# The first FFN layer of three batches by Strassen's seven products, two feature tiles at a time

## The chip, the cores and the metric

The kernel runs on one core of a Trainium2 chip. Its engines are TensorE (PE in the profile, with PEld for its weight loads), VectorE (DVE), ScalarE (ACT), GpSimd (POOL) and SyncE (SP, which issues most DMAs). Each engine takes its own instructions strictly in the order in which the program issues them, and semaphores order the engines among each other. The metric is the device time of one execution in microseconds (us), as the median of several runs.

## The reference: what is computed

For each of 8 batches with 8 heads, S = 512 tokens x of width 64 and 32 state rows are read crosswise, and the result goes through a gated two-layer network (FFN) with weights w_in (512 x 2048) and w_out (2048 x 512):

```python
scores = scale * np.matmul(x, state.transpose(0, 1, 3, 2))
a = np.exp(scores - scores.max(-1, keepdims=True))
a /= a.sum(-1, keepdims=True) + 1e-09
xread = np.matmul(a, state)
# sread: the same with x and state exchanged
x = concatenate([xread, sread], axis=2) as (B * (512 + 32), 512)
h = x @ w_in
g = h * np.cos(h)
return g @ w_out
```

Everything is 32-bit float.

## The kernel before

**The first layer of a batch's tokens.** The read `a @ state` and the multiplication by w_in are joined: `products` (L429) multiplies a batch's state by 512 columns of w_in and keeps the result as an `sw` tile of 128 x 2 x 512 (L433 to L440; two of them alive, four a batch, nt = 0 to 3). The attention weights, transposed, are `aT` of 128 x 2 x 512 (two blocks of 128 heads-and-states, 512 tokens). So the 2048 hidden features of a batch are 16 tiles of 128 features, f = 0 to 15, and tile f is `h = sw[:,0,cols].T @ aT[:,0] + sw[:,1,cols].T @ aT[:,1]`. This is `hidden` (L462), two matmuls into one of two PSUM banks (`hps`, two buffers):

```python
t.hp = hps.tile([P, S], F32, name="h")[:, 0:t.n]
for i in range(t.kn):
    nc.tensor.matmul(out=t.hp, lhsT=t.lhs(i), rhs=t.rhs(i),
                     start=(i == 0), stop=(i == t.kn - 1))
```

**The gate**, h times cos h, follows in four parts: `gate` (ScalarE, L472, rounds h to an integer), `gate2` (VectorE, L475, subtracts), `gate3` (ScalarE, L478, a sine), and `gate4` (VectorE, L484), which takes a slot of `g_all` (28 slots of 128 x 512, a list of free ones taken from the front and refilled at the back) and writes the gated tile there. The bank of `h` is free after `gate4`.

**The second layer** is already done by Strassen's products (in Winograd's form), over a *pair* of batches: phases 0 and 1 are the halves of the 16 tiles of the even batch, phases 2 and 3 those of the odd one. `output` (L603) issues the products of a tile, each two 32-bit matmuls into the banks MAIN or SIDE of `acc`; in phases 0 to 2, for two tiles of three, one product of the pair before is added (`pr.before.more(1)`: p7, then p4). In phases 2 and 3 the sums on the right side are made by `minus` (L490): those called `soon` on VectorE from the second pair on and on GpSimd in the first pair, the others on GpSimd; `sums` is issued after `gate4`, `sums2` later in the step. Finished banks are read by L534 (`plus`), L539 and L541; their stores (`later`, `go` in `store`: L548 sums, L555 transposes and a DMA from SP) follow one by one.

**The order of the work** is written out by hand: a loop over steps (L831), one tile a step, 128 tiles of tokens and then 16 of states. A step issues, in this order: `hidden`; TensorE's attention work of the step (`go(0)`); `gate`, `gate2`; more attention work on ScalarE and VectorE (`go(1)`, `go(3)`); `gate3`; one `later`; `gate4`; `sums`; the rest of attention (`go(2)`, `go(4)`); `blocks` on GpSimd (L816, the sums of w_out, steps 16 to 33); `sums2`; and last `output` of the tile three steps back (LAG, L827). `plan` (L740) puts the parts of the next batch's attention on the 16 steps of the present one: for an even batch from 2 on, transposes L294 in steps 1 and 2, scores (L312) in 5 with the maxima L326, spreading L332 and L349 in 6, L342 and the exponentials L353 and L358 in 7, sums in 8, L379 in 9, transposes L385 in 10, reads L402 in 11 and 12 with L412, and in 15 `keep2` (L418) and `keep3` (L423, which writes the states that were read into `sT`). The `products` of `sw` stand in steps 0, 4 and 9 for this batch, and in step 14 for the first quarter of the next (copied by ScalarE at L439).

**The state tiles** at the end multiply w_in by `sT` (256 columns of all batches) with the same `hidden` and `gate`.

The numbers L... are lines of this text:

Of the kernel before, what the change touches and what calls it, by code (L numbers as in the profile page):

```python
# [21 lines left out]
def kernel(  # L22
# [16 lines left out]
    NC = S // P  # L39
    T = S + Ns  # L40
    WC = 512
    scale = 1.0 / math.sqrt(D)

    consts = ctx.enter_context(tc.tile_pool(name="consts", bufs=1))
# [52 lines left out]

    stT = consts.tile([P, B, P], F32)  # L100

    def load_x(b):

# [111 lines left out]
    def convert_part(i, p):  # L215
# [20 lines left out]
        else:  # L236
            nc.gpsimd.tensor_tensor(bits, bits, e, op=ALU.add)  # L237

    sT = consts.tile([P, NK, B, Ns], F32)
    aT_of, sw_of = {}, {}

    class Attention:

# [4 lines left out]
        def __init__(self, b):  # L250
            self.b = b

            self.x_b, self.xT = x_b, xT
            self.spread, self.z2 = xT[:, 0:2], xT[:, 2:4]
            self.a2T = xT[:, 0:2].rearrange("p j (c m) -> p j c m", c=NC)

            self.i12 = small.tile([P, 2 * self.NB + 2], F32, name="i12")
            self.m1 = self.i12[:, 0:2 * self.NB].rearrange(
                "p (j t) -> p j t", j=2)
            self.i2 = self.i12[:, 2 * self.NB:]  # L260
            self.m2 = small.tile([P, 2], F32, name="m2")
            self.sr = small.tile([P, 2, D], F32, name="sr")
            self.aT = self.z1 = carry.tile([P, 2, S], F32, name="aT")
            aT_of[b] = self.aT

# [155 lines left out]

        def keep3(self):
            nc.scalar.activation(  # L423
                sT[:, :, self.b, :],
                at[1][:, 0:P].rearrange("p (k n) -> p k n", k=NK),
                func=ACTF.Copy, scale=1.0 / TWO_PI)


# [38 lines left out]

    def gate(t):  # L470
        t.q = msb.tile([P, S], F32, name="q")[:, 0:t.n]
        nc.scalar.activation(t.q.bitcast(I32), t.hp, func=ACTF.Copy, bias=0.25)  # L472
# [4 lines left out]
    def gate3(t):  # L477
        nc.scalar.activation(t.q, t.q, func=ACTF.Sin, bias=halfpi,  # L478
                             scale=-TWO_PI)

    def gate4(t):
        t.slot = g_free.pop(0)
        t.g = g_all[:, t.slot, 0:t.n]
        nc.vector.tensor_tensor(t.g, t.hp, t.q, op=ALU.mult)  # L484


# [189 lines left out]
    def tiles():  # L676
        pr = None
        for b in range(B):
            if b % 2 == 0:
                pr = Pair(b // 2, pr)  # L680
            for f in range(NF):
                t = Tile()
                t.b, t.f, t.pair = b, f, pr
                t.phase, t.i = b % 2 * 2 + f // NH, f % NH
                t.n, t.kn = S, 2
                c = slice(P * f % WC, P * f % WC + P)
                t.lhs = lambda i, b=b, nt=P * f // WC, c=c: (
                    sw_of[b, nt][:, i, c])
                t.rhs = lambda i, b=b: aT_of[b][:, i]
                yield t  # L690
        for n in range(NF):
            t = Tile()
            t.b, t.n_th, t.f = B, n, (n + NH) % NF
            t.pair, t.last_pair, t.phase = None, pr, None
            t.n, t.kn = B * Ns, NK
            cols = slice(P * t.f, P * t.f + P)
            t.lhs = lambda i, cols=cols: w_in[:, i, cols]
            t.rhs = lambda i: sT[:, i].rearrange("p b n -> p (b n)")
            yield t


# [38 lines left out]
    def plan(b):  # L740
        pe, x_act, y_act, x_dve, y_dve = [
            {s: [] for s in range(NF)} for _ in range(5)]

        def prod(s, b, nt, *bank):
            pe[s].append((b, "products", nt) + bank)
            if b == 1 and 0 < nt < 3:
                x_dve[s].append((b, "products_taken", nt) + bank)
            else:
                x_act[s].append((b, "products_kept", nt) + bank)

        def pairs(s, b, name, kept, i):
            pe[s] += [(b, name, i), (b, name, i + 1)]
            x_act[s].append((b, kept, i))
            y_act[s].append((b, kept, i + 1))

        def early(b, s):
            if b == 1:
                pairs(s[0], b, "tokens", "tokens_kept", 0)
                pairs(s[1], b, "tokens", "tokens_kept", 2)
            else:  # L760
                for k in range(NK):
                    to = (x_dve, y_dve)[k % 2]
                    to[s[k // 2]].append((b, "tokens_turned", k))
            pe[s[2]].append((b, "scores"))
            x_dve[s[2]].append((b, "max1"))
            x_dve[s[3]].append((b, "spread1"))
            y_dve[s[3]].append((b, "shift"))
            x_dve[s[4]].append((b, "max2"))
            y_act[s[4]].append((b, "exps"))
            x_dve[s[5]].append((b, "sums"))  # L770
            y_dve[s[5]].append((b, "spread1"))
            x_dve[s[6]].append((b, "norm1"))

        def late(b, s):
            pairs(s[0], b, "turn", "turn_kept", 0)
            pe[s[1]].append((b, "reads", 0))
            pe[s[2]].append((b, "reads", 1))
            x_dve[s[2]].append((b, "keep"))
            if len(s) > 3:
                turned(b, s[3])  # L780

        def turned(b, s):
            pe[s].append((b, "keep2"))
            x_act[s].append((b, "keep3"))


        if b == 0:
            pe[0].append((0, "products", 0, SIDE, HC, WC))
            y_dve[0] += [(0, "products_taken", 0, SIDE, HC, WC),
                         (0, "inverse2")]  # L790
            prod(7, 0, 2, SIDE)
            prod(11, 0, 3)
            prod(13, 1, 0, MAIN)
            late(0, (1, 2, 3, 4))
            early(1, (5, 6, 7, 8, 9, 10, 11))
            late(1, (12, 13, 14))
        else:
            bank = (SIDE,) if b == 1 else ()
            if b == 1:
                turned(1, 0)  # L800
            prod(0, b, 1, *[MAIN for _ in bank])
            prod(4, b, 2, *bank)
            prod(9, b, 3, *bank)
            if b + 1 < B:
                prod(14, b + 1, 0)
                early(b + 1, (1 + (b == 1), 2 + (b == 1), 5, 6, 7, 8, 9))
                late(b + 1, (10, 11, 12, 15))
        return pe, x_act, y_act, x_dve, y_dve
# [6 lines left out]
    def blocks(op, out_, a, b, r):  # L815
        nc.gpsimd.tensor_tensor(out_[:, r], a[:, r], b[:, r], op=op)  # L816
# [14 lines left out]
    for step, t in enumerate(all_tiles):  # L831
        s = step % NF
        if s == 0 and t.b < B:
            steps = plan(t.b)
        todo = [p[s] if t.b < B else [] for p in steps]

        def go(n):
            for p in todo[n]:
                part(*p)

        last, conv = conv_at.get(step - 1, -1), conv_at.get(step, -1)
        if step == B * NF + (0 if f64 else 8):
            fetch(N_LOADS + 2)
        if step == 4:
            warm(1, acc[MAIN][0])
        if step != 1:
            hidden(t)
        if step == 0:
            hidden(all_tiles[1])
            warm(3, acc[MAIN][0])  # L850
            gate(t)
            gate2(t)
            convert(3, "bcdf")
            convert(4, "1")
            go(0)
        else:
            go(0)
            if step == 5:
                states(1, acc[SIDE][1])
            gate(t)  # L860
            gate2(t)
            if step == 3:
                warm(4, acc[MAIN][0])
                part(0, "products", 1, SIDE)
            go(1)
            go(3)
            if step == 1:
                convert(4, "bcdf")
            elif last >= 0:
                convert(last, "bcdf")  # L870
            if conv >= 0 and not todo[1]:
                convert(conv, "1")
        gate3(t)
        if step == 3:
            part(0, "products_kept", 1, SIDE)
        if later:
            later.pop(0)()
        gate4(t)
        if conv >= 0 and todo[1] and step > 0:
            convert(conv, "1")  # L880
        if t.pair is not None:
            sums(t)
        if step == 6:
            states_kept(1, acc[SIDE][1])
        go(2)
        if conv >= 0:
            convert(conv, "2")
        go(4)
        if step in block_at:
            blocks(*block_at[step])  # L890
        if t.pair is not None:
            sums2(t)
        while len(line) >= (LAG if step >= 2 * NH else LAG + 1):
            output(line.pop(0))
        line.append(t)
# [32 lines left out]
```

## Time and profile before

| what | us |
|---|---|
| median of 4 runs (774.94 to 776.62) | 775.73 |
| the profiled execution, its own time | 774.7 |
| span of its trace | 772.9 |
| TensorE busy | 761.9 |
| VectorE busy | 414.6 |
| ScalarE busy | 305.7 |
| GpSimd busy | 177.4 |
| batches 2, 4, 6 (`hidden` of their first tile to that of the next batch's), each | 86.8 |
| batches 3 and 5, each | 83.3 |

The span is the time from the first to the last instruction of the traced execution; the 1.8 us around it are launch and end. A line of the groups reads: line, engine, operation, out<-in by the program's names, shapes, xcount | busy us, mean ns of one | idle time of the engine before them and what ended it. A line of the timeline reads: start, duration, engine, line, operation, names, shapes, xcount (instructions in a row are merged) and, in brackets, the idle time before it with its releaser. One 32-bit matmul of the program is two instructions in the trace.

### The profile page before, as it was taken

To read this page: it belongs to the slowest core of one execution; us is meant where nothing else is said; L and a number is where in the kernel's file an instruction comes from. 1 tells how busy PE (TensorE), PEld (TensorE's weight loads), DVE (VectorE), ACT (ScalarE), POOL (GpSimd) and SP (SyncE) were. 2 spreads that over 40 slices of the span, in tenths; PEclk is the share of its full clock that TensorE was granted. 3 is DMA by queue.
4 is the path that set the end of the run, shared out by engine and by line. 5 is a ranking of instruction groups with operands and counts; after the bars stand their busy time and mean duration, and the time that the engine had idled before them with its cause. 6 is when DMAs were issued, how large, how long until landed. Compare 5 with 4: busy or idle time off the path is not lost.

```text
span 772.9 us, 7528 instructions
## 1 busy us (share of the span) xinstructions
PE 761.9 (99%) x2664; PEld 340.2 (44%) x2664; DVE 414.6 (54%) x654; ACT 305.7 (40%) x484; POOL 177.4 (23%) x118
## 2 busy tenths in 40 slices
PE   8998999999999999999999999999999999999997
PEld 3443443434344434434444434444444444455554
DVE  5778786625554468535553658435634546431431
ACT  3888845422263225332342335332533333212112
POOL 2353377862000001640000002630000005510200
PEclk9999999999999999999999999999999999999999
DMA  8595461150104310330105111410100114000021
GB/s 244 170 277 206 129 94 25 21 89 1 27 1 87 50 28 14 55 69 1 28 4 105 28 27 23 86 29 0 28 1 9 23 24 137 0 0 15 14 42 41
DMA packets 161957, 43.49 MB, mean 56 GB/s; under 512 B 153920, under 2 KB 153920, under 8 KB 161920
## 3 DMA queue, kind: packets, MB, share of 16 engines
q1 hardware_dynamic: 161024, 42.49, 25.4%
q10 hardware_dynamic: 768, 0.39, 0.2%
q8 instruction: 21, 0.34, 0.2%
q14 instruction: 16, 0.13, 0.1%
q0 software_dynamic: 128, 0.13, 0.1%
HBM read 34.08 MB, written 8.91 MB: 56 GB/s over the span
## 4 chain that ended last, share of the span: by engine, by line
PE 94%; DVE 3%; ACT 1%; DMA 1%; issue 0%; POOL 0%; SPq 0%; POOLq 0%
PE o L528 50%; PE h L465 31%; PE at L312 4%; PE o L648 4%; PE at L402 2%; PE o L312 1%; PE at L385 1%; DMA x_b<-in_x_dram 1%; DVE i L326 0%; PE o L705 0%; DVE xT L332 0%; DVE w_out L232 0%; DMA s<-in_state_dram 0%; POOL w_out L237 0%; ACT s L226 0%
## 5 line engine op out<-in xcount | busy, mean ns | idle before, releaser
L465 PE MATMUL h<-aT,sw 128*128 128x512 f32 x512 | 241.0, 593 | 2.9 <-DVE g_all L484 2.4
L475 DVE TENSOR_TENSOR q<-q,h 128x512 f32<-128x512 int32 (+1 forms) x144 | 94.4, 656 | 273.6 <-ACT q L472 273.5
L528 PE MATMUL o<-g_all,w_out 128*128 128x512 f32 x512 | 236.4, 598 | 0.3 <-POOL w_out L237 0.3
L472 ACT ACTIVATE q<-h 128x512 int32<-128x512 f32 (+1 forms) x144 | 82.3, 571 | 345.3 <-PE h L465 345.2
L490 POOL TENSOR_TENSOR g_all<-g_all 128x512 f32<-128x512 f32 x80 | 112.7, 1433 | 440.8 <-DVE g_all L484 440.8
L528 PE MATMUL o<-g_all,s 128*128 128x512 f32 x384 | 177.3, 598 | 0.0
L465 PEld LDWEIGHTS h<-aT,sw 128*128 128x128 f32 x512 | 96.6, 190 | 125.8 <-issue 107.6
L528 PEld LDWEIGHTS o<-g_all,w_out 128*128 128x128 f32 x512 | 94.1, 190 | 124.5 <-issue 120.5
L478 ACT ACTIVATE q<-q,halfpi 128x512 f32<-128x512 f32 (+1 forms) x144 | 100.7, 700 | 82.3 <-DVE q L475 82.3
L484 DVE TENSOR_TENSOR g_all<-h,q 128x512 f32<-128x512 f32 (+1 forms) x144 | 94.1, 653 | 55.3 <-ACT q L478 53.5
L528 PEld LDWEIGHTS o<-g_all,s 128*128 128x128 f32 x384 | 70.8, 190 | 91.7 <-issue 90.0
L237 POOL TENSOR_TENSOR w_out<-w_out,s 128x1024 int32<-128x1024 int32 x10 | 23.9, 2391 | 77.1 <-DVE w_out L232 60.3
L490 DVE TENSOR_TENSOR g_all<-g_all 128x512 f32<-128x512 f32 x48 | 33.4, 697 | 1.6
L439 ACT COPY sw<-at 128x512 f32<-128x512 f32 x50 | 26.8, 589 | 10.0 <-PE at L312 10.0
L465 PE MATMUL h<-sT,w_in 128*128 128x256 f32 x128 | 30.2, 379 | 0.0
L648 PE MATMUL o<-w_out,g_all 128*128 128x512 f32 x64 | 29.6, 592 | 0.0
L465 PEld LDWEIGHTS h<-sT,w_in 128*128 128x128 f32 x128 | 24.3, 190 | 10.1 <-issue 6.5
L237 POOL TENSOR_TENSOR w_in<-w_in,s 128x1024 int32<-128x1024 int32 (+1 forms) x10 | 19.3, 1932 | 37.0 <-DVE w_in L232 22.0
L312 PE MATMUL at<-w_in,stT 64*32 64x512 f32 x400 | 27.2, 601 | 0.0
L534 DVE SCALAR_TENSOR_TENSOR held<-o,held 128x512 f32<-128x512 f32 x40 | 25.3, 676 | 3.3 <-PE o L528 3.3
L555 DVE STREAM_TRANSPOSE ot<-held 128x512 f32<-128x512 f32 x32 | 22.2, 693 | 0.0
L332 DVE STREAM_TRANSPOSE xT<-i 128x1024 f32<-128x1024 f32 x16 | 19.8, 1236 | 0.0
(79 smaller groups left out, 405.3 us busy)
## 6 DMA issues: line engine op xcount, KB each, us to landing
out_dram<-ot SPq DMA_DIRECT2D x132, 64.0 KB, 2.0
g_all<-in_moe_w_out_dram SPq DMA_DIRECT2D x8, 1024.0 KB, 4.9
g_all<-in_moe_w_in_dram SPq DMA_DIRECT2D x6, 1024.0 KB, 5.3
xT<-in_x_dram SPq DMA_DIRECT2D x96, 64.0 KB, 2.3
x_b<-in_x_dram SPq DMA_DIRECT2D x24, 256.0 KB, 4.5
x_b<-in_x_dram SPq DMA_DIRECT2D x16, 128.0 KB, 4.1
g_all<-in_moe_w_in_dram SPq DMA_DIRECT2D x4, 512.0 KB, 6.0
x_b<-in_moe_w_out_dram SPq DMA_DIRECT2D x1, 1024.0 KB, 5.3
```

What stands on the lines that cost most here:

```text
L237: nc.gpsimd.tensor_tensor(bits, bits, e, op=ALU.add)
L312: nc.tensor.matmul(out=(to or at)[j][Ns * k:Ns * k + Ns, 0:n], lhsT=w[D * j:D * j + D, self.b, Ns * k:Ns * k + Ns], rhs=r(slice(D * j, D * ...
L439: (copy or nc.scalar.copy)(sw_of[self.b, nt][:, j, c0:c1], to[j][:, 0:c1 - c0])
L465: nc.tensor.matmul(out=t.hp, lhsT=t.lhs(i), rhs=t.rhs(i), start=(i == 0), stop=(i == t.kn - 1))
L472: nc.scalar.activation(t.q.bitcast(I32), t.hp, func=ACTF.Copy, bias=0.25)
L475: nc.vector.tensor_tensor(t.q, t.q.bitcast(I32), t.hp, op=ALU.subtract)
L478: nc.scalar.activation(t.q, t.q, func=ACTF.Sin, bias=halfpi, scale=-TWO_PI)
L484: nc.vector.tensor_tensor(t.g, t.hp, t.q, op=ALU.mult)
L490: engine.tensor_tensor(out, a, b, op=ALU.subtract)
L528: nc.tensor.matmul(out=acc[bank][ch], lhsT=w[:, i, P * ch:P * ch + P], rhs=g.g, start=(i == 0), stop=(i == NH - 1))
L534: nc.vector.scalar_tensor_tensor(out=out.t[:, ch], in0=acc[bank][ch], scalar=TWO_PI, in1=b.t[:, ch], op0=ALU.mult, op1=ALU.add)
L648: nc.tensor.matmul(out=acc[MAIN][i], lhsT=t.g[:, P * i:P * i + P], rhs=w_out[:, :, t.f, :], start=(t.n_th == 0), stop=(t.n_th == NF - 1))
```

## The change

Tiles of batches 2, 4 and 6 (`seven`) are computed by twos, f and f + 1 with f even. The two tiles' weights in `sw` are four blocks of 128 x 128 (`b11`, `b12`, `b21`, `b22`: two features tiles by two blocks of `aT`), and `aT` is four blocks of 128 x 256 (two blocks by two halves of the tokens). Eight block products of 256 columns become seven, in Winograd's form:

- `sw_sums`: four sums of 128 x 128 on GpSimd, issued in the even step before the pair's (one of them in place in `sw`); `halves`: four differences of 128 x 256 on VectorE, once a batch, in step 14 of the batch before.
- `hidden_a`: four products into both PSUM banks, issued in the odd step ahead of the pair, with a ScalarE copy of the first product into the first tile's slot of `g_all`; `sums_a`: three sums on VectorE, after `gate2` of that step.
- `hidden_b`: the other three products, and `sums_b`, two sums on VectorE, at the start of the pair's even step.
- The sums leave both tiles' h in their slots of `g_all`, where the gate reads it and, in place, `gate4` leaves the gated tile. The slots are so taken earlier. The second tile's `gate` stands behind the first one's `gate3`.
- In step 15 of batches 1, 3 and 5, `hidden_a` of the next batch follows that step's own `hidden`, whose result is first copied by ScalarE into its slot to free the bank.
- `products` of the next batch's first quarter go from step 14 to 13, in all batches from 1 on. `sT` shares a tensor with `stT`, shifted by one batch, and is laid out by batch (128 columns each), so that the state tiles read it in eight pieces of 32; `sr` has one buffer in place of two.

```diff
+    st_all = consts.tile([P, B + 1, P], F32)
+    sT = st_all[:, 0:B]
+    stT = st_all[:, 1:B + 1]
...
+    sr = consts.tile([P, 2, D], F32)
+    aS = consts.tile([P, 4, HS], F32)
+    swS = consts.tile([P, 3, P], F32)
...
+    def seven(t):
+        return t.pair is not None and t.b > 1 and t.phase < 2
+
+    def halves(b):
+        aT = aT_of[b]
+        b11, b12 = aT[:, 0, 0:HS], aT[:, 0, HS:S]
+        b21, b22 = aT[:, 1, 0:HS], aT[:, 1, HS:S]
+        for i, x1, x2 in ((0, b12, b11), (1, b22, aS[:, 0]), (2, b22, b12),
+                          (3, b21, aS[:, 1])):
+            nc.vector.tensor_tensor(aS[:, i], x1, x2, op=ALU.subtract)
...
+    def sw_sums(t):
+        b11, b12, b21, b22 = blocks_of(t)
+        t1, t2, t4 = [swS[:, i] for i in range(3)]
+        sub = ALU.subtract
+        for o, x1, x2, op in ((t1, b21, b22, ALU.add), (t2, t1, b11, sub),
+                              (t4, b12, t2, sub), (b21, b11, b21, sub)):
+            nc.gpsimd.tensor_tensor(o, x1, x2, op=op)
...
+    def take_slot(t):
+        t.slot = g_free.pop(0)
+        t.hp = t.g = g_all[:, t.slot, 0:t.n]
+
+    def both(i1, i2):
+        d = i2 - i1
+        ends = slice(i1, i2 + (1 if d > 0 else -1), d)
+        return g_all.rearrange("p t (h s) -> p (t h) s", h=2)[:, ends]
+
+    def hidden_a(t, t2):
+        b11, b12, b21, b22 = blocks_of(t)
+        t.h1, t.h2 = [hps.tile([P, S], F32, name="h") for _ in range(2)]
+        product_of(t.h1[:, LO], b11, aT_of[t.b][:, 0, LO])
+        product_of(t.h1[:, HI], swS[:, 1], aS[:, 1])
+        product_of(t.h2[:, HI], b21, aS[:, 2])
+        product_of(t.h2[:, LO], swS[:, 0], aS[:, 0])
+        take_slot(t)
+        take_slot(t2)
+        t.second = t2
+        nc.scalar.copy(t.g[:, LO], t.h1[:, LO])
+
+    def sums_a(t):
+        t2 = t.second
+        u2, u3 = t.g[:, HI], t2.g[:, LO]
+        e, o = 2 * t.slot, 2 * t2.slot
+        add = nc.vector.tensor_tensor
+        add(u2, t.g[:, LO], t.h1[:, HI], op=ALU.add)
+        add(u3, u2, t.h2[:, HI], op=ALU.add)
+        add(both(o + 1, e + 1), both(o, e + 1),
+            t.h2[:, LO].unsqueeze(1).to_broadcast([P, 2, HS]), op=ALU.add)
+
+    def hidden_b(t):
+        b11, b12, b21, b22 = blocks_of(t)
+        t.h1, t.h2 = [hps.tile([P, S], F32, name="h") for _ in range(2)]
+        product_of(t.h1[:, LO], b12, aT_of[t.b][:, 1, LO])
+        product_of(t.h2[:, HI], swS[:, 2], aT_of[t.b][:, 1, HI])
+        product_of(t.h2[:, LO], b22, aS[:, 3])
+
+    def sums_b(t):
+        e, o = 2 * t.slot, 2 * t.second.slot
+        add = nc.vector.tensor_tensor
+        add(t.g[:, LO], t.g[:, LO], t.h1[:, LO], op=ALU.add)
+        add(both(o, e + 1), both(o, e + 1),
+            t.h2.rearrange("p (h s) -> p h s", h=2), op=ALU.add)
...
-            t.rhs = lambda i: sT[:, i].rearrange("p b n -> p (b n)")
+            t.rhs = lambda i: sT[:, :, Ns * i:Ns * i + Ns]
...
-                prod(14, b + 1, 0)
+                prod(13, b + 1, 0)
...
-        if step != 1:
+        ahead = all_tiles[step + 1:step + 3]
+        if seven(t):
+            if t.f % 2 == 0:
+                hidden_b(t)
+                sums_b(t)
+        elif step != 1:
             hidden(t)
+        first = len(ahead) > 1 and seven(ahead[0]) and ahead[0].f % 2 == 0
+        if first:
+            if not seven(t):
+                h = t.hp
+                take_slot(t)
+                nc.scalar.copy(t.g, h)
+            hidden_a(*ahead)
...
-            gate(t)
+            if not (seven(t) and t.f % 2):
+                gate(t)
             gate2(t)
...
+            if first:
+                sums_a(ahead[0])
             go(1)
             go(3)
...
         gate3(t)
+        if seven(t) and t.f % 2 == 0:
+            gate(t.second)
...
         if step in block_at:
             blocks(*block_at[step])
+        for u in all_tiles[step + 2:step + 3]:
+            if seven(u) and u.f % 2 == 0:
+                if u.f == 0:
+                    halves(u.b)
+                sw_sums(u)
         if t.pair is not None:
             sums2(t)
```

More of the change, by code (lines that the diff above doesn't have):

```diff
@@ L41 @@
     WC = 512
+    HS = S // 2
     scale = 1.0 / math.sqrt(D)
@@ L96 @@
     raw_at = [r.rearrange("p t s -> p (t s)") for r in raw_at]
-    stT = consts.tile([P, B, P], F32)
+    st_all = consts.tile([P, B + 1, P], F32)
+    sT = st_all[:, 0:B]
+    stT = st_all[:, 1:B + 1]
     def load_x(b):
@@ L237, in convert_part @@
             nc.gpsimd.tensor_tensor(bits, bits, e, op=ALU.add)
-    sT = consts.tile([P, NK, B, Ns], F32)
     aT_of, sw_of = {}, {}
+    sr = consts.tile([P, 2, D], F32)
+    aS = consts.tile([P, 4, HS], F32)
+    swS = consts.tile([P, 3, P], F32)
     class Attention:
@@ L261, in __init__ @@
             self.m2 = small.tile([P, 2], F32, name="m2")
-            self.sr = small.tile([P, 2, D], F32, name="sr")
+            self.sr = sr
             self.aT = self.z1 = carry.tile([P, 2, S], F32, name="aT")
@@ L423, in keep3 @@
             nc.scalar.activation(
-                sT[:, :, self.b, :],
-                at[1][:, 0:P].rearrange("p (k n) -> p k n", k=NK),
+                sT[:, self.b], at[1][:, 0:P],
                 func=ACTF.Copy, scale=1.0 / TWO_PI)
@@ L466, in hidden, with blocks_of @@
                              start=(i == 0), stop=(i == t.kn - 1))
+    def seven(t):
[7 more added lines that the diff above has]
+            nc.vector.tensor_tensor(aS[:, i], x1, x2, op=ALU.subtract)
+    def blocks_of(t):
+        sw = sw_of[t.b, P * t.f // WC]
+        c = P * t.f % WC
+        return [sw[:, j, c + P * r:c + P * r + P] for r in range(2)
+                for j in range(2)]
@@ new lines, in sw_sums, with product_of @@
+    def sw_sums(t):
[5 more added lines that the diff above has]
+            nc.gpsimd.tensor_tensor(o, x1, x2, op=op)
+    LO, HI = slice(0, HS), slice(HS, S)
+    def product_of(out, w, r):
+        nc.tensor.matmul(out=out, lhsT=w, rhs=r, start=True, stop=True)
+    def take_slot(t):
+        t.slot = g_free.pop(0)
+        t.hp = t.g = g_all[:, t.slot, 0:t.n]
@@ L481, in gate4 @@
     def gate4(t):
-        t.slot = g_free.pop(0)
-        t.g = g_all[:, t.slot, 0:t.n]
+        if not hasattr(t, "slot"):
+            t.slot = g_free.pop(0)
+            t.g = g_all[:, t.slot, 0:t.n]
         nc.vector.tensor_tensor(t.g, t.hp, t.q, op=ALU.mult)
```

## The prediction

> **What bounds the kernel now.** I read the page first: the busy times, then the chain that ended last, then the costliest groups.
>
> ```profile
> span 772.9 us, 7528 instructions
> PE 761.9 (99%) x2664; PEld 340.2 (44%) x2664; DVE 414.6 (54%) x654; ACT 305.7 (40%) x484; POOL 177.4 (23%) x118
> PE 94%; DVE 3%; ACT 1%; DMA 1%; issue 0%; POOL 0%; SPq 0%; POOLq 0%
> L465 PE MATMUL h<-aT,sw 128*128 128x512 f32 x512 | 241.0, 593 | 2.9 <-DVE g_all L484 2.4
> L475 DVE TENSOR_TENSOR q<-q,h 128x512 f32<-128x512 int32 (+1 forms) x144 | 94.4, 656 | 273.6 <-ACT q L472 273.5
> ```
>
> The reader is to see that TensorE is busy for 99% of the span and is 94% of the chain, while VectorE and ScalarE mostly wait for it (the idle time in front of L475). The granted clock is 9 tenths or more in all 40 slices. So a saved matmul shortens the run, if nothing makes TensorE wait in its place. TensorE's order is fixed, so every wait of its own is lost time: today it has almost none.
>
> The program's 32-bit matmul is two instructions in the trace: 128 tiles x 2 matmuls are 512 rows at L465. A busy time is not a pace, since matmuls overlap, so I take the pace from the timeline of TensorE, at the end of the batches and the start of the state tiles:
>
> ```profile
> 670.43 1.88 PE L465 MATMUL h<-aT,sw 128*128 128x512 f32 x4
> 675.58 1.89 PE L465 MATMUL h<-sT,w_in 128*128 128x256 f32 x8
> ```
>
> Four 512-wide ones take 1.88 us, of which the last is 0.592 long: (1.88 - 0.592)/3 = 0.429 us start to start. Eight 256-wide ones: (1.89 - 0.379)/7 = 0.216. Half the width is half the time, although each has a weight load of 0.190 us (the PEld row of this line) that must fit beside it: 26 ns are left.
>
> **What goes.** A pair of tiles costs 8 x 0.429 = 3.43 us now. Strassen's seven products are 14 instructions of 256 columns: 14 x 0.216 = 3.02. That saves 0.412 us a pair, and 24 pairs (batches 2, 4, 6, eight each) give **-9.9 us**. These weights come from other tiles than in the 256-wide row; if a load did not fit, the pair would lose up to 14 x 0.190 = 2.66 us, but the row that is nearest has the same shape and operand kinds, so I take 0 for this.
>
> The Trainium skill ("TensorE: Matmul & The Clock Gate", Measured speedup vs the span model) says that a weight load overlaps running matmuls only if its row group differs. All loads here use all 128 rows; by that rule a pair would go from 8 x (0.190 + 0.429) to 14 x (0.190 + 0.216), +0.73 us, and the change would cost 17.5 us. The 0.216 pace above speaks against it, and the measurement decides.
>
> **What comes within a batch.** The two banks h1, h2 both belong to one pair, so `hidden_b` waits for `sums_a`, and the next `hidden_a` for `sums_b`. I write T0 for the start of `hidden_a`, T1 of `hidden_b`. A result is readable 0.48 us after its matmul starts (0.379, and 0.10 as between the end of L465 at 349.50 and ACT's L472 at 349.60). VectorE instructions in a row take 0.61 us at 512 wide (four of L534 in 2.44), and 0.34 at 256 (0.422 less the same 0.08 overlap); ScalarE's 256-wide PSUM copy 0.38 (L472, 383 ns).
> - `hidden_a`: 8 x 0.216 = 1.73. h1 is readable at T0+1.13, the copy is done at 1.54, the adds run to 1.91, 2.33 and 3.02 (h2 is readable at 1.99). After it TensorE has at least 1.22 + 1.72 (scores and a step without p7/p4), so `hidden_b` starts no earlier than T0+4.67 and needs h2 0.43 later: 2 us of slack, if VectorE is free.
> - `hidden_b`: 6 x 0.216 = 1.30; h2 readable at T1+1.56, `sums_b` ends at 2.25, `gate` (from SBUF: 0.70, as L478's 512-wide 723 ns and not L472's 595) at 2.98, `gate2` 3.6, `gate3` 4.4, `gate4` 5.1, and the second tile's `gate` at 5.1, so its `gate2` ends at 5.8. `hidden_a` needs h2 at T1+3.02+0.86 at the earliest. Slack again, and a gate's result is used only three steps later (LAG).
>
> What can use up the slack is VectorE's queue. Its worst place is step 2 of a batch, where the four L534 stand:
>
> ```profile
> 358.14 2.44 DVE L534 SCALAR_TENSOR_TENSOR held<-o,held 128x512 f32<-128x512 f32 x4
> 360.53 0.69 DVE L475 TENSOR_TENSOR q<-q,h 128x512 f32<-128x512 int32 x1
> ```
>
> From T1 of step 2: `sums_b` and `gate2` to 3.6, two L294 transposes and `gate4` to 5.7, four L534 to 8.1, `gate2` of the next tile 8.7, `sums_a` to 10.1. TensorE: 1.30 + 3.43 + 1.73 + 3.43 = 9.89 to the next `hidden_b`, whose second product needs h2 at 10.32. Margin 0.2. The SIDE bank that p7 needs at 6.46 is read by 6.4, the first L534: margin 0.1. Around step 8 (L326 1.83 us with its reciprocal, L332 1.2, a table load of 1.28 on ScalarE) the same walk leaves 0.6. Nothing of this is late by itself; extra semaphore instructions (51 ns on TensorE at L465, 21 on VectorE) can make it so. I take 0.3 us a batch, **+0.9**, between 0 and 3.
>
> POOL's `sw_sums` (128-wide: 0.45 each by the line through 1.27 at 512 and 2.36 at 1024, 1.7 for four) is hidden inside a batch: POOL works 2.65 us of the 86.76 us of batch 4. ScalarE's added 24 copies lie under the outputs (busy 31.6 of 86.76).
>
> **What comes at the three entries into batches 2, 4, 6.** Here I expect the loss. In step 15 of the odd batch `hidden_a` stands directly behind `hidden` in TensorE's queue, with no output products between, and its third product needs b21, the fourth instruction of `sw_sums`. That is issued in step 14 on POOL behind step 14's `minus` (L490), which waits for `gate4`. From the timelines of POOL, entry to batch 4 first, then to batch 2:
>
> ```profile
> 335.17 3.00 POOL L490 TENSOR_TENSOR g_all<-g_all 128x512 f32<-128x512 f32 x2 [2.76 <-DVE g_all L484]
> ```
>
> ```profile
> 165.07 3.72 POOL L490 TENSOR_TENSOR g_all<-g_all 128x512 f32<-128x512 f32 x3 [1.98 <-DVE g_all L484]
> 174.50 4.66 POOL L816 TENSOR_TENSOR w_out<-w_out 128x1024 f32<-128x1024 f32 x2
> ```
>
> Batch 4: moving the product of sw from step 14 to 13 shifts step 14's `hidden` 1.22 us later (329.63 to 330.85) and leaves step 15's at 335.99; `gate4` ends 4.83 after it, 335.7. One `minus` follows, 1.77 us long since VectorE's own L490 runs beside it (1.27 without): 337.5. VectorE's `halves` (4 x 0.34) run in this time too; the same slowing (0.50 per 0.65 us of overlap) would add up to 1.05: 338.5. `sw_sums` then ends between 339.2 and 340.3, and with an exposed weight load (0.19) the third product starts at 339.4 to 340.5, where TensorE would be ready at 335.99 + 1.72 + 0.86 = 338.57. The wait is 0.85 to 1.9; I take 1.4, and the same for batch 6. Batch 2: both `minus` of sums run on POOL (2.47 us from 165.65) and none on VectorE: b21 at 169.9 to 170.9, due at 168.48, wait 1.6 to 2.65, I take 2.1. There L816 (2.33 each) also stands ahead of the `sw_sums` for step 33: 0 to 0.9 more, I take 0.3. Sum: **+5.2** (3.3 to 7.4). The other need at the entry, the copy of tile 15 out of its bank, is done by 338.6 and so not last.
>
> The Trainium skill ("SBUF — State Buffer", Who interferes with whom) has a stricter price: a VectorE instruction with two SBUF inputs and a GpSimd one block each other fully. By it b21 would come at about 340.7 and batches 4 and 6 would lose 0.9 us more each.
>
> **Small edits.** The sw product (PE 1.22 us, two ScalarE copies) only changes its step; it passes no DMA, and SP's and POOL's queues keep their order but for the sums above. State tiles read `sT` in pieces of 32: L402 reads pieces of 64 at full pace (8 pairs in 0.82 us, beside 0.87 for 8 at L385), so 0; its single duration is 279 against 273 ns, and 6 ns for each of seven more pieces in 128 matmuls would be 5.4 us, the upper end. `sr` single: its uses are a batch apart, 0. The profiled execution took 774.7 for its span of 772.9; the median of the runs shown is 775.73, 1.0 above. -9.9 + 0.9 + 5.2 = **-3.8**: span 769.1, profiled 770.9, median **772.0**.
>
> **Rivals.**
> 1. *The entries cost little*: POOL and VectorE share better than I think, the waits are at their lower ends, and nothing is lost within batches: 775.7 - 9.9 + 3.3 = **769.1**. For: POOL's small-instruction price is extrapolated. Against: the order on POOL's queue. 0.13.
> 2. *A near wash*: entries at their upper end and 1.0 a batch within: -9.9 + 7.4 + 3.0 = +0.5, about **776**. 0.14.
> 3. *Slower: TensorE waits for h at each pair*, because VectorE reaches `sums_a` or `sums_b` late. VectorE's work in batch 4 rises from 42.6 us by 8 x (1.29 + 0.95) + 1.4 to 62 of some 84. With the entries paid, 4.7 us are left, so it decides from 0.2 us a pair on; one more 256-wide add late in each (0.34 x 24 = 8.2) gives 775.7 - 4.7 + 8.2 = **779**. For: margins of 0.1 and 0.2. Against: only one step of a batch has them. 0.18.
> 4. *The interleaved writes of `both` are ordered as one range* over all slots between: then output products wait for the adds, 1.3 + 1.0 us a pair in some 17 pairs whose slots lie apart (by the order of the free list): up to 39 us, some **800**. 0.04.
>
> The forecast has 0.51, and is faster throughout (770 to 774). A difference under 0.2%, 1.6 us, can't be told from none. Faster 0.64; same 0.14; slower 0.22. The range of 767 to 779 takes in cases 1 and 2 and the milder half of 3, and leaves out 4 and the tails.
>
> **What would show it.** Right: seven products in rows of 256 at 0.216, TensorE idle before the third product of an entry, released by POOL, 1 to 2.7 us three times, and hardly elsewhere. Wrong: idle time of L465's successors released by the adds on VectorE in many pairs (3), idle before L528 (4), a 256-wide pace above 0.216, or no idle at the entries (1).

## The result, and the profile after

The changed kernel takes 774.25 us (median of 35 runs, 772.85 to 776.25) against 775.88 for the kernel before (56 runs). The ratio is 0.9977, interval [0.9972, 0.9983]: 1.6 us less, where 3.8 were forecast. The page of the kernel after, its lines that answer to those of before:

```profile
span 773.0 us, 8101 instructions
PE 757.7 (98%) x2808; PEld 366.6 (47%) x2808; DVE 487.2 (63%) x786; ACT 314.1 (41%) x511; POOL 227.7 (29%) x214
PE 89%; DVE 4%; POOL 3%; ACT 2%; DMA 1%; issue 1%; SPq 0%; DVEq 0%; ACTq 0%; POOLq 0%
L471 PE MATMUL h<-aT,sw 128*128 128x512 f32 x320 | 151.3, 596 | 2.9 <-DVE g_all L573 2.4
L507 PE MATMUL h<-aS,swS 128*128 128x256 f32 x96 | 29.0, 383 | 3.6 <-POOL swS L502 3.6
L507 PE MATMUL h<-aS,sw 128*128 128x256 f32 x96 | 29.0, 383 | 1.5 <-POOL sw L502 1.5
```

TensorE is busy 4 us less, VectorE is busy 73 us more, and the chain, once 94% TensorE, now runs 3% through GpSimd. The two products that read GpSimd's sums have idle time in front of them, released by GpSimd.

The spans of the two profiled executions are equal (772.9 and 773.0) although the medians differ. The windows of the kernel after show why:

```profile
72.00:74.70 2.70, 1.14 (x3) 0.66 (x4) 1.58 (x3) 2.68 (x7) 1.65 (x1) 1.00 0.16 7
74.80:78.10 3.30, 3.30 (x19) 0.33 (x17) 3.23 (x7) 2.30 (x3) 0.61 (x1) 0.50 0.80 310
78.20:82.00 3.80, 3.80 (x12) 1.84 (x13) 3.55 (x5) 3.58 (x5) 0.00 (x0) 1.00 0.00 0
```

After the window's length come the busy times of PE, PEld, DVE, ACT and POOL, the granted clock and the DMA figures. Behind a wait of some 2 us in batch 0, which both kernels have (1.95 us idle, up to 73.56 and 73.13 us), TensorE got half its clock for a little over three microseconds in this execution; the profile of before happened to have no such stretch. So I compare the part that changes: from the `hidden` of step 31 to the first state tile it is 675.58 - 165.90 = 509.68 us before and 676.00 - 167.65 = 508.35 after, 1.33 less. For the same stretch I list below what TensorE loses, as the start-to-start time of neighbouring matmuls over their pace (0.216 at 256 columns, 0.429 at 512).

The timeline of TensorE after, the entry to batch 2 and step 33:

```profile
167.65 1.88 PE L471 MATMUL h<-aT,sw 128*128 128x512 f32 x4
169.36 0.59 PE L507 MATMUL h<-aT,sw 128*128 128x256 f32 x2
171.43 0.70 PE L507 MATMUL h<-aS,swS 128*128 128x256 f32 x2 [1.47 <-POOL swS L502]
172.38 0.70 PE L507 MATMUL h<-aS,sw 128*128 128x256 f32 x2 [0.25 <-POOL sw L502]
172.91 0.59 PE L507 MATMUL h<-aS,swS 128*128 128x256 f32 x2
...
176.89 0.59 PE L507 MATMUL h<-aT,sw 128*128 128x256 f32 x2
177.32 0.60 PE L507 MATMUL h<-aT,swS 128*128 128x256 f32 x2
177.75 0.59 PE L507 MATMUL h<-aS,sw 128*128 128x256 f32 x2
...
182.83 0.59 PE L507 MATMUL h<-aT,sw 128*128 128x256 f32 x2
184.66 0.70 PE L507 MATMUL h<-aS,swS 128*128 128x256 f32 x2 [1.23 <-POOL swS L502]
185.61 0.70 PE L507 MATMUL h<-aS,sw 128*128 128x256 f32 x2 [0.25 <-POOL sw L502]
```

A product in step (176.89, 177.32, 177.75) takes 0.43 us, two matmuls of 0.215: the pace of the forecast. At 169.36 and at 182.83 the second and third product wait for swS and sw from GpSimd. Also the two matmuls of the product after a wait start 0.32 us apart instead of 0.216: in the trace its weight load starts only with it (171.43), where otherwise it starts 0.43 us ahead (168.93 for the product at 169.36). All losses of the stretch:

| where | forecast, us | lost, us |
|---|---|---|
| entry to batch 2 (step 31) | 2.1 | 2.25 |
| step 33, sums behind the block sum of w_out | 0.3 | 2.01 |
| entries to batches 4 and 6, each | 1.4 | 1.49 |
| steps 4 and 10 of batches 2, 4, 6, all | 0.9 | 1.25 |
| sum | 6.1 | 8.5 |

Saved matmuls less losses: -9.9 + 8.5 = -1.4, and 1.33 us is measured on the stretch.

GpSimd's timeline after shows what is ahead of the sums:

```profile
167.41 2.78 POOL L579 TENSOR_TENSOR g_all<-g_all 128x512 f32<-128x512 f32 x2 [1.95 <-DVE g_all L573]
170.15 0.63 POOL L502 TENSOR_TENSOR swS<-sw 128x128 f32<-128x128 f32 x1
170.86 0.52 POOL L502 TENSOR_TENSOR swS<-swS,sw 128x128 f32<-128x128 f32 x1
...
176.39 3.73 POOL L579 TENSOR_TENSOR g_all<-g_all 128x512 f32<-128x512 f32 x3 [2.83 <-DVE g_all L573]
180.08 2.80 POOL L905 TENSOR_TENSOR w_out<-w_out 128x1024 f32<-128x1024 f32 x1
182.84 0.90 POOL L502 TENSOR_TENSOR swS<-sw 128x128 f32<-128x128 f32 x1
183.83 0.78 POOL L502 TENSOR_TENSOR swS<-swS,sw 128x128 f32<-128x128 f32 x1
```

The small sums (L502) wait behind `minus` (L579), which waits for `gate4` (L573); in step 32 the block sum (L905) stands between as well. And the instructions are longer than they are alone: L905 2.80 us instead of 2.36, the sums 0.90 and 0.78 instead of 0.45. VectorE, at the same time:

```profile
179.77 0.90 DVE L563 TENSOR_TENSOR q<-q,g_all 128x512 f32<-128x512 int32 x1 [0.70 <-ACT q L560]
181.46 1.98 DVE L573 TENSOR_TENSOR g_all<-g_all,q 128x512 f32<-128x512 f32 x1 [0.79 <-ACT q L566]
183.36 0.94 DVE L563 TENSOR_TENSOR q<-q,g_all 128x512 f32<-128x512 int32 x1
```

Here `gate2` and `gate4` read both inputs from SBUF, since h now lies in `g_all`, and take 0.90 to 1.98 us where 0.69 is usual. The trace holds its own comparison: of the 96 small sums, the 53 that overlap with no VectorE instruction with two SBUF inputs take 0.46 us or less, although 41 of them run beside some other VectorE instruction; of the 43 that do overlap with one, 32 take longer, up to 0.90. And `gate4` of the plain tiles, with h in PSUM, never takes more than 0.69, with GpSimd at work beside it (30 of 77) or not. The prediction counted this slowing for `minus` and `halves` alone.

### The profile page after: what moved, and what is told of

It reads as the page before. It is cut to its first block, busy times and chain, and to the rows that moved or that the text cites. A ratio compares the mean times of both kernels' runs of the same rounds, so it can differ in the third digit from the quotient of the medians.

```text
span 773.0 us, 8101 instructions
## 1 busy us (share of the span) xinstructions
PE 757.7 (98%) x2808; PEld 366.6 (47%) x2808; DVE 487.2 (63%) x786; ACT 314.1 (41%) x511; POOL 227.7 (29%) x214
## 4 chain that ended last, share of the span: by engine, by line
PE 89%; DVE 4%; POOL 3%; ACT 2%; DMA 1%; issue 1%; SPq 0%; DVEq 0%; ACTq 0%; POOLq 0%
PE o L617 48%; PE h L471 20%; PE h L507 9%; PE at L319 4%; PE o L737 4%; PE at L409 2%; POOL g_all L579 1%; PE o L319 1%; POOL swS L502 1%; PE at L392 1%; DVE q L563 1%; DMA x_b<-in_x_dram 1%; ACT q L560 1%; DVE g_all L573 1%; ACT q L566 0%
## 5 line engine op out<-in xcount | busy, mean ns | idle before, releaser
L617 PE MATMUL o<-g_all,w_out 128*128 128x512 f32 x512 | 236.4, 598 | 0.3 <-POOL w_out L242 0.3
L579 POOL TENSOR_TENSOR g_all<-g_all 128x512 f32<-128x512 f32 x80 | 113.1, 1435 | 247.9 <-DVE g_all L573 247.9
L617 PE MATMUL o<-g_all,s 128*128 128x512 f32 x384 | 177.3, 598 | 0.0
L563 DVE TENSOR_TENSOR q<-q,h 128x512 f32<-128x512 int32 (+1 forms) x93 | 59.5, 640 | 160.6 <-ACT q L560 160.6
L471 PE MATMUL h<-aT,sw 128*128 128x512 f32 x320 | 151.3, 596 | 2.9 <-DVE g_all L573 2.4
L617 PEld LDWEIGHTS o<-g_all,w_out 128*128 128x128 f32 x512 | 93.9, 190 | 119.3 <-issue 115.4
L560 ACT ACTIVATE q<-h 128x512 int32<-128x512 f32 (+1 forms) x93 | 52.0, 559 | 206.7 <-PE h L471 206.6
L617 PEld LDWEIGHTS o<-g_all,s 128*128 128x128 f32 x384 | 70.8, 190 | 88.5 <-issue 86.3
L471 PEld LDWEIGHTS h<-aT,sw 128*128 128x128 f32 x320 | 60.2, 190 | 79.5 <-issue 66.2
L573 DVE TENSOR_TENSOR g_all<-h,q 128x512 f32<-128x512 f32 (+1 forms) x93 | 59.3, 637 | 35.0 <-ACT q L566 34.6
L560 ACT ACTIVATE q<-g_all 128x512 int32<-128x512 f32 x51 | 31.8, 623 | 90.6 <-DVE g_all L553 90.2
L563 DVE TENSOR_TENSOR q<-q,g_all 128x512 f32<-128x512 int32 x51 | 37.6, 738 | 21.7 <-ACT q L560 21.7
L573 DVE TENSOR_TENSOR g_all<-g_all,q 128x512 f32<-128x512 f32 x51 | 37.3, 732 | 10.5 <-ACT q L566 10.4
L502 POOL TENSOR_TENSOR swS<-sw 128x128 f32<-128x128 f32 x24 | 11.9, 496 | 82.0 <-PE h L507 66.9
L579 DVE TENSOR_TENSOR g_all<-g_all 128x512 f32<-128x512 f32 x48 | 33.5, 697 | 1.6
L507 PE MATMUL h<-aS,swS 128*128 128x256 f32 x96 | 29.0, 383 | 3.6 <-POOL swS L502 3.6
L507 PE MATMUL h<-aS,sw 128*128 128x256 f32 x96 | 29.0, 383 | 1.5 <-POOL sw L502 1.5
L471 PE MATMUL h<-st_all,w_in 128*128 128x256 f32 x128 | 30.2, 379 | 0.0
```

Source lines behind the costliest of these rows:

```text
L471: nc.tensor.matmul(out=t.hp, lhsT=t.lhs(i), rhs=t.rhs(i), start=(i == 0), stop=(i == t.kn - 1))
L507: nc.tensor.matmul(out=out, lhsT=w, rhs=r, start=True, stop=True)
L563: nc.vector.tensor_tensor(t.q, t.q.bitcast(I32), t.hp, op=ALU.subtract)
L579: engine.tensor_tensor(out, a, b, op=ALU.subtract)
L617: nc.tensor.matmul(out=acc[bank][ch], lhsT=w[:, i, P * ch:P * ch + P], rhs=g.g, start=(i == 0), stop=(i == NH - 1))
```

## The experiments

My theory after the result: the saving is whole (9.9 us), and what is missing is TensorE waiting for GpSimd's small sums at four places. Rivals: contention of the two engines for SBUF makes the sums late wherever they stand; VectorE's adds hold the banks at every pair; a small edit has a cost of its own. "Stretch" is the time from step 31's `hidden` to the first state tile in the profiled execution (before 509.68, after 508.35).

**The entries' sums early.** At the top of step 14, ahead of `minus` in GpSimd's queue:

```diff
+        for u in all_tiles[step + 2:step + 3]:
+            if seven(u) and u.f == 0:
+                halves(u.b)
+                sw_sums(u)
         ahead = all_tiles[step + 1:step + 3]
...
-            if seven(u) and u.f % 2 == 0:
-                if u.f == 0:
-                    halves(u.b)
+            if seven(u) and u.f % 2 == 0 and u.f > 0:
                 sw_sums(u)
```

> The changed kernel, but at the three entries the GpSimd sums and the VectorE differences of the next batch are issued at the top of step 14, ahead of that step's minus instead of behind it. Theory (the time that is missing is waiting of TensorE for GpSimd's queue at the entries): the trace of the changed kernel shows 2.25 us lost at the entry of batch 2 and 1.48 each at batches 4 and 6, 5.2 in all; they go, the ratio to the kernel before falls from 0.9977 to about 0.991 (769 us). Rival (contention of VectorE and GpSimd for SBUF makes the sums long, wherever they stand): the sums stay long and half or less of it goes, ratio 0.994 or more.

Ratio 0.9922 [0.9909, 0.9934], 769.12 us; stretch 504.30, 4.1 less than after. TensorE's wait for the sums is gone at the three entries. What is left there is 0.48 at batch 2, where TensorE waits for the copy of tile 15 out of its bank and that copy for a `minus` on GpSimd, and 0.20 each at 4 and 6, where the trace names no releaser and the same copy ends just before; step 33's loss grew to 2.3. So 4.1 in place of 5.2, as these two terms say, and more than half: the theory's side. The sums at the entry to batch 4 stayed as long as the rival says (0.63, 0.52, 0.52, 0.45), but they are early now.

**The small sums ahead of the block sum** in step 32 (and in every step):

```diff
-        if step in block_at:
-            blocks(*block_at[step])
         for u in all_tiles[step + 2:step + 3]:
...
                 sw_sums(u)
+        if step in block_at:
+            blocks(*block_at[step])
```

> The changed kernel, but in step 32 the four small GpSimd sums are issued ahead of the large GpSimd block sum of w_out instead of behind it. Theory: the 2.0 us that TensorE loses in step 33 go, and nothing else changes: 2.0 us less, ratio 0.995. Rival (the wait comes from the late gate of tile 31, not from the block): the same 0.9977.

Ratio 0.9958 [0.9944, 0.9971], 1.5 us below the 0.9977 of after. Step 33 has no wait for GpSimd left in the trace, though `gate4` of tile 31 is no earlier; 0.45 us of another wait came in step 35, where the output waits for the four plus instructions. The rival falls. The stretch of the profiled execution does not show the gain (508.56, 0.2 more than after), since some 1.7 us of half clock fell behind its entry to batch 2; that also makes TensorE later at step 33, so the next run, which has no half clock there, is the cleaner trace.

**Both reorderings.**

> Both reorderings together. Theory: 7.2 us less than the changed kernel, 0.9977 - 0.0093 = 0.988, about 767 us; what is left is 9.9 us of matmuls saved less 1.3 us of small waits within the batches. Rival (a queue that is relieved moves the wait to the next late thing, VectorE's adds): 0.991 or more.

Ratio 0.9894 [0.9881, 0.9907], 767.61 us; stretch 502.17, that is 6.2 less than after and 7.5 less than before. Step 33 loses 0.1 here. Of the 1.0 us that is missing from the theory's 7.2, 0.87 is the copy of tile 15 at the three entries: a next wait did appear, a small one. The entry to batch 4 in TensorE's timeline:

```profile
333.78 1.88 PE L471 MATMUL h<-aT,sw 128*128 128x512 f32 x4
335.50 0.59 PE L507 MATMUL h<-aT,sw 128*128 128x256 f32 x2
335.93 0.59 PE L507 MATMUL h<-aS,swS 128*128 128x256 f32 x2
336.49 0.67 PE L507 MATMUL h<-aS,sw 128*128 128x256 f32 x2
336.99 0.59 PE L507 MATMUL h<-aS,swS 128*128 128x256 f32 x2
```

The products follow each other at 0.43 to 0.56 us, with no idle time named. 2.2 us of losses remain in the stretch, and -9.9 + 2.2 = -7.7 against the 7.5 measured. This version is faster than both kernels; of the versions here, only the last one below can't be told apart from it.

**The small edits alone.** `seven` returns False, all else as after:

```diff
-        return t.pair is not None and t.b > 1 and t.phase < 2
+        return False
```

> The kernel before with the small edits alone: the product of sw in step 13, the state tensor laid out by batch and shared, one buffer for sr; no tile by Strassen's products. Theory: no difference, ratio 1.000 within 0.0005. Rival (the state tiles' reads in pieces of 32 cost up to 6 ns for each piece): up to +5.4 us, 1.007.

Ratio 0.9997 [0.9987, 1.0007]; stretch 509.68, to the hundredth that of before, and 97.33 us from the first state tile on, against 97.35. The moved product, the layout of `sT` and the single `sr` cost nothing.

**`halves` two steps earlier**, the GpSimd sums left late:

```diff
+        for u in all_tiles[step + 4:step + 5]:
+            if seven(u) and u.f == 0:
+                halves(u.b)
         ahead = all_tiles[step + 1:step + 3]
...
-                if u.f == 0:
-                    halves(u.b)
                 sw_sums(u)
```

> The changed kernel, with one edit: VectorE's four differences of aT for the next batch are issued at the top of step 12 instead of the end of step 14; GpSimd's small sums stay where they are. It tells how much of the entry wait is contention of the two engines for SBUF. Theory (the order of GpSimd's queue is most of it, contention stretches it): the small sums shrink from 0.5 to 0.6 us each to 0.45, each entry wait falls by 0.4 to 0.7 us, 1.5 us in all, ratio 0.9958. If contention were the whole wait: 5.2 us less, 0.991. If it were none: 0.9977.

Ratio 0.9958 [0.9945, 0.9972]; stretch 506.83, 1.5 less. GpSimd at the entry to batch 4, where the kernel after had 0.63, 0.52, 0.52 and 0.63:

```profile
338.00 1.77 POOL L579 TENSOR_TENSOR g_all<-g_all 128x512 f32<-128x512 f32 x1 [2.73 <-DVE g_all L573]
339.73 0.45 POOL L502 TENSOR_TENSOR swS<-sw 128x128 f32<-128x128 f32 x1
340.26 0.46 POOL L502 TENSOR_TENSOR swS<-swS,sw 128x128 f32<-128x128 f32 x1
340.79 0.45 POOL L502 TENSOR_TENSOR swS<-sw,swS 128x128 f32<-128x128 f32 x1
341.20 0.45 POOL L502 TENSOR_TENSOR sw<-sw 128x128 f32<-128x128 f32 x1
```

So contention is real, and that with `halves` is some 30% of the loss at the entries, 1.5 us of 5.2: 0.5 of 2.25 at batch 2 and of 1.49 at 4 and 6. The rest is the order of the queue, with a `minus` ahead that still takes 1.77 us in place of 1.27 at batches 4 and 6; no run parts the two.

**One add more in each pair** (the first line of `sums_a` twice):

```diff
         add(u2, t.g[:, LO], t.h1[:, HI], op=ALU.add)
+        add(u2, t.g[:, LO], t.h1[:, HI], op=ALU.add)
```

> The changed kernel, with the first 256-wide add of each sums_a issued twice (0.34 us more of VectorE ahead of the freeing of both banks, in each of 24 pairs). Theory (VectorE's lateness bites only in the two steps of a batch where it bites now, 3 and 9; in the others there is slack of 1 us or more): 2 x 3 x 0.34 = 2.0 us more at most, ratio 1.0003. Rival 3 of the prediction (the wait for h stands at every pair): 24 x 0.34 = 8.2 us more, 1.008.

Ratio 1.0049 [1.0035, 1.0063], 5.6 us over the kernel after: between the two. The profiled execution (stretch +5.2) lost 1.7 us of it to half clock behind the entry to batch 2. Of the rest, the two steps that the theory names cost 4.4, more than double its 2.0, and the entry to batch 4 0.4; step 33 gave back 1.2, since TensorE came to it later. TensorE's waits of this kernel:

```profile
PE h L507 <- DVE g_all L540: 3.0, 6, 0.6
PE h L507 <- POOL swS L502: 2.8, 3, 1.5
```

Six waits for VectorE's adds, two in each batch, in steps 4 and 10 (the theory names them by the step of the adds, 3 and 9) and in no others: the rival of a wait at every pair falls. But step 10 rose from 0.23 to 1.2 us a batch, not by 0.34. The extra add of step 7 makes ScalarE wait 0.61 us for the maxima (none in the kernel after), its next `gate` comes 0.8 us later against TensorE, and from there VectorE has no pause up to the adds of step 9, where the second extra add comes on top.

**`sums_a` ahead of `gate2`**, on both reorderings:

```diff
+            if first and seven(t):
+                sums_a(ahead[0])
             gate2(t)
...
-            if first:
+            if first and not seven(t):
                 sums_a(ahead[0])
```

> Both reorderings, and sums_a issued ahead of gate2 of its step instead of behind it (in the batches by seven products). Theory: the small waits of 0.19 and 0.23 us in steps 4 and 10, 0.42 a batch, go: 1.3 us less than both reorderings alone, 0.9894 - 0.0016 = 0.988. Rival (gate2 now waits for TensorE and the gates come late three steps on): 0.990 or more.

Ratio 0.9932 [0.9919, 0.9944]: 2.9 us slower than both reorderings alone. The wait in step 4 went, but that in step 10 rose from 0.23 to 0.9 us, and in batch 2 the output of step 35 waited 1.1 us for the four plus instructions. In step 7, `gate2` now stands behind `sums_a`, so ScalarE's sine and with it the exponentials start later; the next `gate` follows them on ScalarE (220.28 us), VectorE waits 2.1 us for it, and the sums of step 9 come that much later. The theory for this edit was wrong.

**An eighth product**, on both reorderings (the last line of `hidden_b` twice):

```diff
         product_of(t.h2[:, LO], b22, aS[:, 3])
+        product_of(t.h2[:, LO], b22, aS[:, 3])
```

> Both reorderings, and the last product of hidden_b issued twice, so that a pair has eight 256-wide products like a plain block product. It measures what one product is worth. Theory (TensorE's pace is the price: 2 x 0.216 us a product): 24 x 0.432 = 10.4 us more, ratio 0.9894 + 0.0134 = 1.003. Rival (part of a product's time was hidden in waits anyway): 5 us more or less than that, 0.996 or below.

Ratio 1.0015 [1.0006, 1.0024], 9.4 us over both reorderings; stretch +9.5. The 10.4 of the pace less 0.8 of waits that the later banks hide (1.4 us lost instead of 2.2) is 9.6. A 256-wide product is worth its 0.43 us.

**Seven products in phase 2 too**, on both reorderings:

```diff
-        return t.pair is not None and t.b > 1 and t.phase < 2
+        return t.pair is not None and t.b > 1 and t.phase < 3
```

> Both reorderings, and the seven products also for the first eight tiles of batches 3, 5 and 7 (phase 2): 12 pairs more. TensorE's pace gives 12 x 0.41 = 4.9 us. Theory (what decides is VectorE's queue, which in these batches has the minus of phase 2 too, and the step with the four plus instructions at their start): some of it is lost to waits for the two banks, 0.5 to 1 us a batch, so 2 to 3.5 us less than both reorderings alone, ratio 0.985 to 0.987. Rival (VectorE is full in these batches, every pair waits): nothing gained or slower, 0.990 or more.

Ratio 0.9994 [0.998, 1.0007]. TensorE's waits at the entry to batch 5, with the windows behind them:

```profile
419.62 0.70 PE L507 MATMUL h<-aT,swS 128*128 128x256 f32 x2 [0.84 <-POOL swS L502]
421.17 0.70 PE L507 MATMUL h<-aS,sw 128*128 128x256 f32 x2 [0.85 <-DVE aS L488]
421.70 5.29 PE L617 MATMUL o<-g_all,w_out 128*128 128x512 f32 x8
```

```profile
416.00:422.00 6.00, 4.31 (x19) 2.03 (x12) 4.47 (x9) 1.69 (x3) 2.29 (x4) 1.00 0.89 167
422.20:425.50 3.30, 3.30 (x5) 1.23 (x4) 2.36 (x5) 1.87 (x3) 0.00 (x0) 0.50 0.72 118
```

Two waits of 0.84 and 0.85 us, and behind them eight matmuls took 5.29 us instead of 3.60, at a granted clock of 0.50. The wait itself comes from sums that were issued one product too early: they overwrite sums that are still to be read, so this version computes the last pair of batches 2, 4 and 6 wrongly, and its time tells only of the waits. The same version with the sums in the right place:

```diff
         elif step != 1:
             hidden(t)
+        for u in all_tiles[step + 2:step + 3]:
+            if seven(u) and u.f == 0:
+                halves(u.b)
+                sw_sums(u)
```

> The version with phase 2 once more, but the early sums are issued behind hidden_b of step 14 instead of ahead of it. (In the version before, the sums of an odd batch overwrote those that hidden_b of step 14 still had to read, so that the last pair of batches 2, 4 and 6 was computed from the wrong sums.) Its trace showed 2.0 us lost at each entry to an odd batch, where TensorE waited for those sums, two stretches of half clock behind them, and 1.3 us in steps 8 and 9 of the odd batches, where hidden waits for gate4. Theory (sums in time cost nothing, what is left is VectorE's queue): the entries' 6 us and the half clock go, 4.9 - 2.6 = 2.3 us less than both reorderings alone, ratio 0.986. Rival (the entry to an odd batch stays late, since its sums now wait for hidden_b and stand behind sums_b): 0.992 or more.

Ratio 0.9884 [0.9868, 0.9901], 766.45 us. The stretch is 500.18, 2.0 less than both reorderings alone, near the 2.3 expected, and the trace shows why it is not 4.9: 1.5 us are lost in each of batches 3 and 5, where `hidden` waits for `gate4` on VectorE. 4.9 less 3.0 is 1.9. (The waits stand in steps 10 and 11 of these batches, not in 8 and 9 as the expectation has it.) By the ratios the gain over both reorderings (0.001) lies inside the intervals: unclear.

## Why the prediction was wrong

- **What bounds the kernel, and the saving**: right. Pace 0.215, no weight load in the way, 9.9 us saved; the eighth product confirms the price.
- **The entries**: the mechanism, its places and its releaser were right, and the three entries cost 5.2 us where 4.9 were forecast (2.1 + 1.4 + 1.4). Part of the wait, at batch 2 most of it (1.47 of idle time against 0.25), stands in front of the second product, for `swS`; the prediction named the third alone, which waits on for b21. The stricter price that the prediction names, 0.9 us more at each of batches 4 and 6, did not come: 1.49 was lost there. VectorE was held up more: beside a `minus` on GpSimd, one 256-wide difference took 1.49 us where 0.41 is usual, without TensorE waiting for it.
- **The step that failed** is the last term of that part: "There L816 (2.33 each) also stands ahead of the `sw_sums` for step 33: 0 to 0.9 more, I take 0.3". It measured 2.01, and this is 1.7 of the 2.4 us by which the losses were underrated. The order was seen, the size was not: the prediction gives no walk for this term, as it does for the entries. The block sum and the small sums ran 1.2 us longer than alone (2.80 for 2.36, 0.90 and 0.78 for 0.45), because `gate2` and `gate4` of the tiles by seven products read both inputs from SBUF and meet GpSimd there; the prediction had put this slowing on `minus` and `halves` alone. Without it some 0.8 would be left (an estimate, 2.01 less 1.2), inside its 0 to 0.9 but above its 0.3. Taking the block out of the way removed the wait; that the slowing is 1.2 of it is read from the trace, and no run takes the slowing away alone.
- **Within a batch**: 1.25 for 0.9, in the step-4 place that the walk through VectorE's queue named, and in step 10, where it had left 0.6. The extra add showed how thin these margins are.
- **Small edits**: right, 0.
- The rule on weight loads that the prediction takes from the Trainium skill ("TensorE: Matmul & The Clock Gate", where it stands under The mechanism) would have made the change 17.5 us slower; the rows of L507, 0.43 us a product, speak against it here too. The same section has a second case in which a load runs ahead, into the background weight buffer, which the prediction leaves out; no run here tells which case this is.
- Rival 3 did not come, rival 4 neither: the kernel after has no idle time in front of the output products (L617) in the stretch.

In sum, losses of 8.5 in place of 6.1 left 1.4 of a forecast 3.8. When a saving and its losses nearly cancel, an error of 40% in the losses is more than half of the difference.

## What to carry to other kernels

A saving on the bounding engine is real only as far as the inputs of the new instructions are early. For every new instruction look at what is queued ahead of its producer, and for whom that waits: here two changes of issue order on an engine with 70% idle time turned a gain of 1.6 us into one of 8.2. An operand moved from PSUM to SBUF can slow an engine that does not read it: here `gate2` and `gate4`, with both inputs in SBUF, and GpSimd's sums slowed each other, and with h in PSUM they had not.

## What the runs showed of the hardware

- Behind waits with 1.7 to 2 us of idle time, TensorE's granted clock fell to 0.50 for 3.41 us in some executions, and at the same place of the program not in others (at 74.78 us in the kernel after, not there with both reorderings): some 1.7 us lost beyond the wait. Where one trace has two such stretches or more, their starts lie whole multiples of 3.413 us apart (98.99 us with the small sums ahead of the block sum, 29 times; 348.16 and 170.67 with the first version of phase 2, 102 and 50 times). The Trainium skill ("TensorE: Matmul & The Clock Gate", What's actually happening) has free-running windows of 3413 ns, which agrees with this. It puts the half clock behind an idle window of some 3.4 us; here less idle time was enough in some executions.
- A VectorE instruction with two SBUF inputs and GpSimd instructions slow each other in both directions: GpSimd's 128-wide sum took 0.45 us alone and up to 0.90, VectorE's 512-wide product 0.69 alone and up to 1.98.
